# Polysketch attention and a gated FFN on one core: another way to load and spread S, and another order of the first loads

## The chip, the cores and the metric

The kernel runs on one core of a Trainium2 chip. The time is the device time in microseconds of one execution; a kernel's time is the median of several. Before the change it is 306.29 us (median of 4 runs, 305.91 to 307.54).

## What is computed

Two blocks follow each other. The first is attention with polynomial sketches, for 4 batches, 4 heads, 1088 tokens and a head dimension of 32; the second is a gated feed-forward block on the 4352 tokens with 128 features, with 1536 inner features.

```python
def phi(x):                                   # r = 8
    a = np.einsum('rd,bhsd->bhsr', S1, x)
    b = np.einsum('rd,bhsd->bhsr', S2, x)
    return np.einsum('bhsi,bhsj->bhsij', a, b).reshape(*x.shape[:-1], r * r)
q_p, k_p = (phi(q), phi(k))
kv = np.einsum('bhsf,bhsd->bhfd', k_p, v)
z = np.sum(k_p, axis=2)
num = np.einsum('bhsf,bhfd->bhsd', q_p, kv)
den = np.einsum('bhsf,bhf->bhs', q_p, z)[..., None] + 1e-06
x = (num / den), heads side by side            # (4352, 128)
gate = 1.0 / (1.0 + np.exp(-(x @ w_gate)))
out = gate * (x @ w_val) @ w_out
```

q, k and v come as float32. S1, S2 (8 x 32 each) and the three weights come as float64 (they were divided by a square root), so their bytes are twice those of float32 and the kernel turns them into float32 itself.

## The kernel before

The steady part is the feed-forward block. The 4352 tokens go through in nine chunks (eight of 512, one of 256). For each chunk and each of 12 blocks j of 128 inner features, TensorE makes the two products for gate and val (`w1`, L354, tile `wave`), ScalarE the sigmoid (L362), VectorE the product of both (L375, tile `g`), and TensorE adds the block's share of the output (`w2`, L311, tile `moeout`). The attention of batches 1 to 3 is laid in between these, a piece at a time (`slot`, L389 and following, and the loop at the end).

The attention of batch 0 has nothing to hide behind. It is written out by hand, and each engine runs its instructions in the order in which the code makes them (the schedule is manual). The first microseconds are therefore a chain:

- Loads. Queue of SyncE: `load_s` (L130), the second piece of k, the first of q, v in four transfers (`load_v`), then the weights of blocks 0 and 1 (`load_w(0)`: gate, val, out), the rest of q, and the weights of the other block pairs. Queue of ScalarE: the first piece of k alone. SyncE's queue waits, from the eighth transfer or so on, for the landing of the transfer eight before it.
- `warm` (L246): products of ones, made only to keep TensorE at work; three of 512 columns at the start (L256) and one of 256 later (L840). A float32 product runs as two passes.
- S. `load_s` reads each of S1 and S2 sixteen times, so that all 128 partitions hold a row (`sr_in`). `narrow` (L83) makes float32 of float64 in steps: on VectorE L97, L105 and L109, on ScalarE L101 and L117, on POOL L118, and on VectorE L121, which writes `sr`. Then VectorE transposes it in blocks of 32 (L784, `st`) and masks it by head into `sk` (L788). `sk` is the stationary side of `kps` (L442), the first real product; ScalarE spreads `st` into `s0` and `s1` (L804) for q.
- k and q. VectorE turns k (`turn_k`, L419, in two pieces) and q (`turn_q`, L430). `kps` makes k's sketches, VectorE turns them (`kab`, L452) and multiplies them out (`kp`, `outer`, L521). `ab` (L549, L568) does q's. `gram` (L465, L488) makes the sum z in another way, `dn` (L721, L740) the denominator and numerator, `kv0` (L629, tile `kvz`) k's features times v, `kvd` (L665) and `ndt` (L699, L712) bring that into the form for the numerator, and `divide` writes the first 512 tokens of `xT` (L767), with which the feed-forward block starts.
- Weights. `narrow_01` makes float32 of blocks 0 and 1: part 0 is gate and val of block 0, part 1 of block 1, part 2 the two of w_out. Its first steps stand on ScalarE and POOL (L101, L97) behind `gs` and `gh` of `gram`. `narrow_w` does the later blocks, a block per wave.

The order of `kv0`'s products before: the first 20 right behind `spread_z` (L821), ahead of `dps` (L721), and the last 16 in `rest` (L830), behind the second half of `outer`.

Of the kernel before, what the change touches and what calls it, by code (L numbers as in the profile page):

```python
# [8 lines left out]
F32 = mybir.dt.float32  # L9
I32 = mybir.dt.int32  # L10
U32 = mybir.dt.uint32
I64 = mybir.dt.int64
ALU = mybir.AluOpType
ACTF = mybir.ActivationFunctionType
MUL = ALU.mult

P = 128
# [3 lines left out]
def kernel(  # L21
# [12 lines left out]
    nc = tc.nc  # L34

    B, H, S, D = q.shape
    R = S1.shape[0]
# [6 lines left out]
    T = S // 32  # L44

    NJK = 9
    KBASE = [0, 9, 17, 25]
    assert T == 34
    TCH = 512
    tok_chk = [(o, min(TCH, NTOK - o)) for o in range(0, NTOK, TCH)]  # L50

    const = ctx.enter_context(tc.tile_pool(name="const", bufs=1))
# [3 lines left out]
    sbN = ctx.enter_context(tc.tile_pool(name="sbN", bufs=1))  # L56
# [5 lines left out]
    pso = ctx.enter_context(tc.tile_pool(name="pso", bufs=1, space=bass.MemoryType.PSUM))  # L62
# [17 lines left out]
    wide = S1.dtype == I64  # L80
    assert all((a.dtype == I64) == wide for a in (S2, moe_w_gate, moe_w_val, moe_w_out))

    def narrow(out, bits, eng, bank=None):  # L83

        n, m = out.shape[1:]
        lo, hi = bits[:, :, :, 0].bitcast(U32), bits[:, :, :, 1]

        def tmp(dt, tag, bufs):
            return sbN.tile([P, 3, P], dt, tag=tag, name=tag, bufs=bufs)[:, :n, :m]

        cap, tail = tmp(I32, "cap", 6), tmp(I32, "tail", 5)
        eng.tensor_scalar(  # L97
            out=cap.bitcast(F32), in0=hi.bitcast(F32), scalar1=122880.0, scalar2=-122880.0,
            op0=ALU.min, op1=ALU.max,
        )  # L100
        nc.scalar.activation(out=tail, in_=lo, func=ACTF.Copy, scale=2.0**-29)  # L101
        yield

        head = tmp(I32, "head", 3)
        nc.vector.tensor_scalar(  # L105
            out=head, in0=cap, scalar1=3, scalar2=0x3FFFFFF8,
            op0=ALU.logical_shift_left, op1=ALU.bitwise_and,
        )
        nc.vector.scalar_tensor_tensor(  # L109
            out=head, in0=cap, scalar=-0x40000000, in1=head, op0=ALU.bitwise_and, op1=ALU.bitwise_or  # L110
        )
        yield
        square = cap.bitcast(F32)
        if bank:
            square = pso.tile([P, 512], F32, tag=bank, name="square")[:, : n * m]
            square = square.rearrange("p (n m) -> p n m", n=n)
        nc.scalar.activation(out=square, in_=cap.bitcast(F32), func=ACTF.Square)  # L117
        nc.gpsimd.tensor_tensor(out=head, in0=head, in1=tail, op=ALU.add)  # L118
        yield

        nc.vector.scalar_tensor_tensor(  # L121
            out=out, in0=square, scalar=1.265625 * 2.0**-30, in1=head.bitcast(F32),
            op0=ALU.is_ge, op1=MUL,
        )
        yield

    sr = const.tile([P, 2, D], F32, tag="sr", name="sr")
    sr_in = const.tile([P, 2, D, 2], I32, tag="sr_in", name="sr_in") if wide else None

    def load_s():  # L130
        for n, s_ in enumerate((S1, S2)):
            rows = bass.AP(tensor=s_.tensor, offset=s_.offset, ap=[[0, P // R], [D, R], [1, D]])
            if wide:
                nc.sync.dma_start(
                    out=sr_in[:, n].rearrange("p d w -> p (d w)"), in_=rows.bitcast(I32)
                )
            else:
                nc.sync.dma_start(out=sr[:, n], in_=rows)


    w_sb = const.tile([P, 3, NJ, P], F32, tag="w_sb", name="w_sb")
    w_in = {}

    def load_w(n):
        j0, j1 = 2 * n, 2 * n + 2
        cs = slice(j0 * P, j1 * P)
        if wide:
            w_in[n] = raw.tile([P, 3, 2, P, 2], I32, tag="w_in", name="w_in")
        for i, src in enumerate((moe_w_gate, moe_w_val)):
            if wide:  # L150
                nc.sync.dma_start(
                    out=w_in[n][:, i].rearrange("p j m w -> p (j m w)"),
                    in_=src[:, cs].bitcast(I32),
                )
            else:
                nc.sync.dma_start(
                    out=w_sb[:, i, j0:j1].rearrange("p j m -> p (j m)"), in_=src[:, cs]
                )
        src = moe_w_out[cs, :].bitcast(I32) if wide else moe_w_out[cs, :]
        nc.sync.dma_start(  # L160
            out=w_in[n][:, 2].rearrange("p j m w -> p j (m w)") if wide else w_sb[:, 2, j0:j1],
            in_=src.rearrange("(j p) m -> p j m", p=P),
        )
# [28 lines left out]
    def load_rows(src, b, t, parts=((0, T, nc.sync),)):  # L192
        for t0, t1, eng in parts:
            eng.dma_start(
                out=t[:, t0:t1, :],
                in_=bass.AP(
                    tensor=src.tensor,
                    offset=src[b, 0].offset + t0 * D,
                    ap=[[T * D, P], [1, (t1 - t0) * D]],
                ),  # L200
            )

    def load_v(b):
        t = ld.tile([P, H, NJK, D], F32, tag="v", name="v")
        base = v[b, 0].offset
        for g in range(4):
            nc.sync.dma_start(
                out=t[32 * g : 32 * g + 32],
                in_=bass.AP(
                    tensor=v.tensor,  # L210
                    offset=base + KBASE[g] * D,
                    ap=[[T * D, 32], [S * D, H], [1, NJK * D]],
                ),
            )
        return t

    k_t, q_t, v_t = {}, {}, {}
# [11 lines left out]
            load_rows(q, b, q_t[b])  # L229

    new_kq(0)
    load_rows(k, 0, k_t[0], ((0, KBASE[2] + 1, nc.scalar),))
    load_s()
    load_rows(k, 0, k_t[0], ((KBASE[2] + 1, T, nc.sync),))
    load_rows(q, 0, q_t[0], ((0, T0, nc.sync),))
    v_t[0] = load_v(0)
    load_w(0)
    load_rows(q, 0, q_t[0], ((T0, T, nc.sync),))
    for n in range(1, NJ // 2):
        load_w(n)  # L240

    ones = const.tile([P, 32], F32, tag="ones")
    nc.vector.memset(ones, 1.0)
# [2 lines left out]
    def warm(*cols):  # L246
        t = psm.tile([P, 2, 512], F32, tag="wave", name="warm")
        one = [bass.AP(tensor=ones.tensor, offset=ones.offset, ap=[list(ones.ap[0]), [0, n]]) for n in cols]
        x = bass.AP(tensor=ones.tensor, offset=ones.offset, ap=[list(ones.ap[0]), [0, P]])
        for r in one:  # L250
            n = r.shape[-1]
            nc.tensor.matmul(out=t[:, 0, :n], lhsT=x, rhs=r, start=True, stop=True)  # L252

    sig0 = const.tile([P, 1], F32, tag="sig0")
    nc.scalar.activation(out=sig0, in_=ones[:, :1], func=ACTF.Sigmoid)
    warm(512, 512, 512)  # L256
    hm = const.tile([P, 2, R], F32, tag="hm")
    nc.vector.memset(hm, 0.0)  # L258
    for h in range(H):
# [1 line left out]
    ident = const.tile([P, P], F32, tag="ident")  # L261
# [9 lines left out]
    for c in range(2):  # L271
        rows = slice(64 * c, 64 * c + 64)
        nc.vector.tensor_reduce(
            out=m_col[rows, c],
            in_=ident[rows].rearrange("p (k j) -> p j k", j=R),
# [3 lines left out]
    for t, x in (  # L279
# [5 lines left out]
        out=e_sum,  # L285
        in_=bass.AP(
            tensor=e_row.tensor,
            offset=e_row.offset,
            ap=[list(e_row.ap[0]), [0, 2], [1, R], [0, R]],
        ),  # L290
# [332 lines left out]
    def kv0(j_list):  # L623
        if 0 not in KVZ:
            KVZ[0] = pso.tile([P, TCH], F32, tag="acc0", name="kvz")
        for j in j_list:
            kr = 64 if j == 0 else P
            for h in range(H):
                nc.tensor.matmul(  # L629
                    out=KVZ[0][32 * h : 32 * h + 32, :F],  # L630
                    lhsT=v_t[0][:kr, h, j, :],
                    rhs=KP[0][:kr, h // 2, j, h % 2, :],
                    start=(j == 1),
                    stop=(j == NJK - 1),
                    skip_group_check=True,
                )
# [78 lines left out]
    def dn(b, n, mid=None):  # L715
# [58 lines left out]

        return divide

    steps = narrow(sr, sr_in, nc.vector) if wide else iter(())
    turn_k(0, 0, KBASE[2] + 1)
    for _ in range(3):
        next(steps, None)  # L780
    turn_k(0, KBASE[2] + 1, T)
    next(steps, None)
    st_ = const.tile([P, 2, 4, R], F32, tag="st", name="st")
    nc.vector.transpose(  # L784
        out=st_.rearrange("p n u r -> p (n u r)"), in_=sr.rearrange("p n d -> p (n d)")
    )
    sk = const.tile([P, 2, 2, R], F32, tag="sk")
    nc.vector.tensor_tensor(  # L788
        out=sk,
        in0=st_[:, :, :2].rearrange("p n m r -> p m n r"),  # L790
        in1=bass.AP(
            tensor=hm.tensor, offset=hm.offset, ap=[list(hm.ap[0]), [R, 2], [0, 2], [1, R]]
        ),
# [24 lines left out]
    spread_z()  # L818
    for pi in range(2):
        outer(0, pi, 0, 5)  # L820
    kv0([1, 2, 3, 4, 0])  # L821
    mult00()
    mult10()
    mask_z()


    def rest(turn, rc, dT):
        for pi in range(2):
            outer(0, pi, 5, NJK)
        kv0(range(5, NJK))  # L830
        turn()
        nt = rc.shape[1] - 1
        nc.scalar.activation(out=rc[:, :nt], in_=dT[:, :nt, :2], func=ACTF.Identity, bias=eps)
        kvd(0)
        narrow_01(0, 1)
        narrow_01(0, 2)
        ndt(0)
# [100 lines left out]
```

## Time and profile before

| | us |
|---|---|
| median of 4 runs | 306.29 |
| the profiled execution | 307.54 |
| its span | 305.6 |
| TensorE busy | 297.5 (97%) |
| VectorE busy | 155.8 (51%) |
| ScalarE busy | 80.7 (26%) |
| POOL busy | 34.7 (11%) |
| `wave` products (L354) | 192.1 |
| `moeout` products (L311) | 105.5 |
| start of the first `kps` product | 7.11 |
| start of the first `wave` product | 16.97 |

Times of events are counted from the start of the span. The busy time of TensorE counts a pass until its modelled end; passes overlap, so the distance from the start of one pass to that of the next tells more than its length. A row of the clock tells which share of TensorE's full speed was granted; the stretch before the first record of a clock (here before 4.68 us) is shown as 1.00.

### The profile page before, as it was taken

Reading aid. Unit: us, or ns where it says so; the run is one execution under the profiler, and the core shown is the slowest. Engines: PE = TensorE matmul, PEld = TensorE weight load, DVE = VectorE, ACT = ScalarE, POOL = GpSimd, SP = SyncE. Lnnn points to the kernel's source line nnn. Section 1 sums busy time; section 2 is a strip of 40 time slices with the busy share of each in tenths; the row PEclk is TensorE's granted clock in tenths of the full one; section 3 lists DMA queues with packets and bytes.
Section 4 is the critical chain, followed back from the end, with each engine's and each line's share of the span. In section 5 each row is a group of like instructions: output and inputs, shape, how many; then the busy total and the mean of one; then the engine's idle time right before and its main releaser. Section 6 shows DMA issues by size and latency. Waiting matters only on the chain.

```text
span 305.6 us, 3603 instructions
## 1 busy us (share of the span) xinstructions
PE 297.5 (97%) x1361; PEld 137.2 (45%) x1361; DVE 155.8 (51%) x268; ACT 80.7 (26%) x150; POOL 34.7 (11%) x63
## 2 busy tenths in 40 slices
PE   6799999999999999999999999999999999999994
PEld 2454434444344444443444444434444444444683
DVE  6988888853846544563465542645232223222331
ACT  3455542221123222212222222221222222222220
POOL 2355550320000400000004100000000000000000
PEclk9989999999999999999999999999999999999999
DMA  6993531599502490341005950200011000100011
GB/s 194 349 344 72 133 118 42 115 170 171 156 0 34 108 222 20 69 150 42 0 5 130 169 81 2 35 0 2 0 17 17 0 0 8 28 0 0 7 28 17
DMA packets 29841, 23.35 MB, mean 76 GB/s; under 512 B 21184, under 2 KB 24768, under 8 KB 29824
## 3 DMA queue, kind: packets, MB, share of 16 engines
q1 hardware_dynamic: 25600, 15.54, 19.0%
q0 software_dynamic: 3456, 7.09, 12.8%
q10 hardware_dynamic: 768, 0.51, 0.7%
q8 instruction: 10, 0.16, 0.2%
q14 instruction: 7, 0.06, 0.1%
HBM read 19.86 MB, written 3.26 MB: 76 GB/s over the span
## 4 chain that ended last, share of the span: by engine, by line
PE 87%; DMA 6%; DVE 2%; POOL 1%; SPq 1%; issue 1%; ACT 0%; DVEq 0%; ACTq 0%
PE wave L354 53%; PE moeout L311 28%; DMA bq<-dq 4%; PE nps L740 2%; PE dps L721 1%; DMA kq<-in_k_dram 1%; PE kps L442 1%; PE kvz L643 1%; DMA out_dram<-o_sb 1%; PE cqps L588 1%; POOL qp L612 1%; POOL bq L612 0%; DVE qp L621 0%; SPq L332 0%; DVE kp L521 0%
## 5 line engine op out<-in xcount | busy, mean ns | idle before, releaser
L354 PE MATMUL wave<-xT,w_sb 128*128 128x512 f32 (+1 forms) x436 | 192.1, 567 | 0.0
L375 DVE TENSOR_TENSOR g<-wave,sg 128x512 f32<-128x512 f32 x102 | 70.4, 690 | 130.4 <-ACT sg L362 130.1
L354 PEld LDWEIGHTS wave<-xT,w_sb 128*128 128x128 f32 x436 | 83.4, 191 | 93.1 <-issue 88.7
L362 ACT ACTIVATE sg<-wave 128x512 f32<-128x512 f32 x102 | 60.9, 597 | 202.7 <-PE wave L354 202.7
L311 PE MATMUL moeout<-g,w_sb 128*128 128x512 f32 (+1 forms) x216 | 105.5, 576 | 0.1
L311 PEld LDWEIGHTS moeout<-g,w_sb 128*128 128x128 f32 x216 | 39.5, 190 | 44.1 <-issue 38.4
L612 POOL DMA_DIRECT2D qp<-dq x12 | 7.0, 587 | 109.5 <-DMA dq<-cq 109.5
L118 POOL TENSOR_TENSOR head<-head,tail 128x384 int32<-128x384 int32 (+2 forms) x14 | 13.4, 960 | 19.5 <-DVE head L109 14.7
L621 DVE TENSOR_TENSOR qp<-qp,bq 128x1152 f32<-128x1152 f32 (+1 forms) x7 | 9.1, 1295 | 4.2 <-DMA bq<-dq 4.2
L521 DVE TENSOR_TENSOR kp<-kab 128x1152 f32<-128x1152 f32 (+2 forms) x10 | 10.9, 1110 | 0.0
L109 DVE SCALAR_TENSOR_TENSOR head<-cap,head 128x384 int32<-128x384 int32 (+2 forms) x14 | 7.5, 538 | 0.5
L321 DVE STREAM_TRANSPOSE o_sb<-moeout 128x512 f32<-128x512 f32 (+1 forms) x9 | 6.1, 680 | 2.6 <-PE moeout L311 2.5
L612 POOL DMA_DIRECT2D bq<-dq x12 | 6.9, 577 | 0.5 <-DMA out_dram<-o_sb 0.2
L252 PE MATMUL warm<-ones 128*128 128x512 f32 (+1 forms) x8 | 5.9, 887 | 1.0 <-DVE hm L258 1.0
L101 ACT ACTIVATE tail<-w_in 128x384 int32<-128x384 uint32 (+1 forms) x13 | 6.5, 521 | 1.0 <-DMA w_in<-in_moe_w_val_dram 1.0
L97 POOL TENSOR_SCALAR cap<-w_in 128x384 f32<-128x384 f32 (+1 forms) x13 | 6.5, 506 | 0.5 <-DMA w_in<-in_moe_w_val_dram 0.5
L121 DVE SCALAR_TENSOR_TENSOR w_sb<-square,head 128x384 f32<-128x384 f32 (+1 forms) x11 | 5.6, 518 | 1.7 <-POOL head L118 1.6
L767 DVE TENSOR_TENSOR xT<-nps,rb 128x576 f32<-128x576 f32 (+2 forms) x9 | 5.9, 661 | 0.8
L740 PE MATMUL nps<-qp,nd 64*32 64x256 f32 (+1 forms) x128 | 6.0, 432 | 0.4 <-ACT nd L712 0.4
L756 DVE STREAM_TRANSPOSE rb<-rc 128x576 f32<-128x576 f32 (+2 forms) x9 | 6.1, 681 | 0.3
L419 DVE STREAM_TRANSPOSE kT<-kq 128x1088 f32<-128x1088 f32 (+2 forms) x5 | 5.4, 1072 | 1.2 <-DMA kq<-in_k_dram 1.2
L430 DVE STREAM_TRANSPOSE qT<-kq 128x512 f32<-128x512 f32 (+1 forms) x8 | 5.8, 720 | 0.0
(72 smaller groups left out, 83.3 us busy)
## 6 DMA issues: line engine op xcount, KB each, us to landing
qp<-dq POOLq DMA_DIRECT2D x12, 288.0 KB, 8.2
bq<-dq POOLq DMA_DIRECT2D x12, 288.0 KB, 8.4
v<-in_v_dram SPq DMA_DIRECT2D x16, 144.0 KB, 5.0
kq<-in_k_dram SPq DMA_DIRECT2D x3, 544.0 KB, 3.9
kq<-in_q_dram SPq DMA_DIRECT2D x3, 544.0 KB, 5.4
w_in<-in_moe_w_gate_dram SPq DMA_DIRECT2D x6, 256.0 KB, 5.8
w_in<-in_moe_w_val_dram SPq DMA_DIRECT2D x6, 256.0 KB, 6.1
w_in<-in_moe_w_out_dram SPq DMA_DIRECT2D x6, 256.0 KB, 6.6
```

Of the source, the lines that this page charges most:

```text
L97: eng.tensor_scalar(out=cap.bitcast(F32), in0=hi.bitcast(F32), scalar1=122880.0, scalar2=-122880.0, op0=ALU.min, op1=ALU.max,)
L101: nc.scalar.activation(out=tail, in_=lo, func=ACTF.Copy, scale=2.0**-29)
L109: nc.vector.scalar_tensor_tensor(out=head, in0=cap, scalar=-0x40000000, in1=head, op0=ALU.bitwise_and, op1=ALU.bitwise_or)
L118: nc.gpsimd.tensor_tensor(out=head, in0=head, in1=tail, op=ALU.add)
L311: nc.tensor.matmul(out=moe["acc"][:, :tw], lhsT=w_sb[:, 2, j, :], rhs=g[:, jj, :tw], start=(j == 0), stop=(j == NJ - 1),)
L354: nc.tensor.matmul(out=wv[:, which, jj * tw + o : jj * tw + o + tp], lhsT=w_sb[:, which, j0 + jj, :], rhs=xT[:, t0 + o : t0 + o + tp], sta ...
L362: nc.scalar.activation(out=sg, in_=wv[:, 0], func=ACTF.Sigmoid)
L375: nc.vector.tensor_tensor(out=g, in0=wv[:, 1], in1=sg, op=MUL)
L521: nc.vector.tensor_tensor(out=KP[b][:, pi, j0:j1].rearrange("p j m (i l) -> p (j m) i l", i=R), in0=bass.AP(tensor=a0.tensor, offset=a0.of ...
L612: get.dma_start(out=t[64 * c : 64 * c + 64, n * H * W1 : (n + 1) * H * W1], in_=bass.AP(tensor=d0.tensor, offset=d0.offset, ap=rows + [[1, ...
L621: nc.vector.tensor_tensor(out=q0, in0=q0, in1=half(BQ[b], n), op=MUL)
L740: nc.tensor.matmul(out=t[32 * h : 32 * h + 32, c, :w], lhsT=ND[b][rows, 32 * h : 32 * h + 32], rhs=half(QP[b], n)[rows, 2 * (h % 2) + h // ...
```

## The change

S is read once: S1 onto partitions 0 to 7 and S2 onto 8 to 15 (`s_in`). `narrow` works on these 16 partitions, and its last step writes four copies side by side (`s4`, 16 x 4 x 32). One TensorE product with the identity turns and spreads them in one go into PSUM (128 x 16, in bank `acc0`), where `sk` and the two copies of ScalarE read it. The block transposition on VectorE is gone. The first three steps of `narrow` stand ahead of the first turn of k on VectorE instead of behind it, and the step that writes `s4` stands ahead of the second turn.

The second piece of k goes onto ScalarE's queue, behind the first. `load_w` is split: gate and val of blocks 0 and 1 stand ahead of v on SyncE's queue, and w_out behind v as before. The first 20 products of `kv0` move behind `dps`. The first `warm` has two products instead of three.

```diff
-    def narrow(out, bits, eng, bank=None):
+    def narrow(out, bits, eng, bank=None, copies=None):
-        n, m = out.shape[1:]
+        p, n, m = bits.shape[:3]
...
+        head = head.bitcast(F32)
+        if copies:
+            square, head = (
+                bass.AP(tensor=x.tensor, offset=x.offset, ap=[list(x.ap[0]), [0, copies], [1, m]])
+                for x in (square, head)
+            )
         nc.vector.scalar_tensor_tensor(
-            out=out, in0=square, scalar=1.265625 * 2.0**-30, in1=head.bitcast(F32),
-            op0=ALU.is_ge, op1=MUL,
+            out=out, in0=square, scalar=1.265625 * 2.0**-30, in1=head, op0=ALU.is_ge, op1=MUL
         )
...
-    sr = const.tile([P, 2, D], F32, tag="sr", name="sr")
-    sr_in = const.tile([P, 2, D, 2], I32, tag="sr_in", name="sr_in") if wide else None
+    s4 = const.tile([2 * R, 4, D], F32, tag="s4", name="s4")
+    s_in = const.tile([2 * R, 1, D, 2], I32, tag="s_in", name="s_in") if wide else s4[:, :1]
     def load_s():
         for n, s_ in enumerate((S1, S2)):
-            rows = bass.AP(tensor=s_.tensor, offset=s_.offset, ap=[[0, P // R], [D, R], [1, D]])
+            rows = s_in[R * n : R * n + R, 0]
             if wide:
-                nc.sync.dma_start(
-                    out=sr_in[:, n].rearrange("p d w -> p (d w)"), in_=rows.bitcast(I32)
-                )
+                nc.sync.dma_start(out=rows.rearrange("p d w -> p (d w)"), in_=s_.bitcast(I32))
...
     new_kq(0)
-    load_rows(k, 0, k_t[0], ((0, KBASE[2] + 1, nc.scalar),))
     load_s()
-    load_rows(k, 0, k_t[0], ((KBASE[2] + 1, T, nc.sync),))
+    load_rows(k, 0, k_t[0], ((0, KBASE[2] + 1, nc.scalar), (KBASE[2] + 1, T, nc.scalar)))
     load_rows(q, 0, q_t[0], ((0, T0, nc.sync),))
+    load_w_in(0)
     v_t[0] = load_v(0)
-    load_w(0)
+    load_w_out(0)
     load_rows(q, 0, q_t[0], ((T0, T, nc.sync),))
     for n in range(1, NJ // 2):
-        load_w(n)
+        load_w_in(n)
+        load_w_out(n)
...
-    warm(512, 512, 512)
+    warm(512, 512)
...
-    steps = narrow(sr, sr_in, nc.vector) if wide else iter(())
+    if wide:
+        steps = narrow(s4, s_in, nc.vector, copies=4)
+        for _ in range(3):
+            next(steps)
     turn_k(0, 0, KBASE[2] + 1)
-    for _ in range(3):
-        next(steps, None)
+    if wide:
+        next(steps)
...
     turn_k(0, KBASE[2] + 1, T)
-    next(steps, None)
-    st_ = const.tile([P, 2, 4, R], F32, tag="st", name="st")
-    nc.vector.transpose(
-        out=st_.rearrange("p n u r -> p (n u r)"), in_=sr.rearrange("p n d -> p (n d)")
-    )
+    st_ = pso.tile([P, TCH], F32, tag="acc0", name="st")
+    nc.tensor.matmul(
+        out=st_[:, : 2 * R],
+        lhsT=s4.rearrange("p g d -> p (g d)"),
+        rhs=ident[: 2 * R, : 2 * R],
+        is_transpose=True,
+        start=True,
+        stop=True,
+    )
+    st_ = st_[:, : 2 * R].rearrange("p (n r) -> p n r", n=2)
...
     for pi in range(2):
         outer(0, pi, 0, 5)
-    kv0([1, 2, 3, 4, 0])
     mult00()
...
     def rest(turn, rc, dT):
+        kv0([1, 2, 3, 4, 0])
         for pi in range(2):
             outer(0, pi, 5, NJK)
```

## The prediction

> **What bounds the kernel now.** I read the page first, then the chain of waits of the first 30 us, then the same stretch engine by engine in order of time, then windows with the granted clock.
>
> ```profile
> span 305.6 us, 3603 instructions
> PE   6799999999999999999999999999999999999994
> PE 87%; DMA 6%; DVE 2%; POOL 1%; SPq 1%; issue 1%; ACT 0%; DVEq 0%; ACTq 0%
> ```
>
> From the third slice on (15 us) TensorE is never idle, and its work there is not touched by the diff. So the change is worth what it moves in the first 17 us, before the first `wave` matmul (16.97 us), and no more. The chain of waits there:
>
> ```profile
> 1.49 0.58 SPq L134
> 2.07 0.05 issue
> 2.12 3.59 DMA kq<-in_k_dram
> 5.71 0.02 issue
> 5.73 0.08 DVE kT L419
> 5.81 0.56 issue
> 6.37 0.19 DVE sr L121
> 6.58 0.26 DVE st L784
> 6.86 0.20 DVE sk L788
> 7.11 0.72 PE kps L442 x16
> ```
>
> Columns are start, length, what. The second piece of k is issued at 2.12, behind the two S transfers on SyncE's queue, and lands at 5.71. Then VectorE does four things one after another (turn of k, `sr`, `st`, `sk`) and `kps` starts at 7.11.
>
> ```profile
> 1.16 1.28 ACT L255 ACT_TABLE_LOAD   x1 [1.16 <-PEq L922]
> 3.58 0.78 DVE L419 STREAM_TRANSPOSE kT<-kq 128x576 f32<-128x576 f32 x1 [0.89 <-DMA kq<-in_k_dram]
> 3.68 0.34 PEld L252 LDWEIGHTS warm<-ones 128*128 128x128 f32 x1 [0.52 <-issue]
> 4.53 0.26 PEld L252 LDWEIGHTS warm<-ones 128*128 128x128 f32 x1 [0.52 <-issue]
> 4.78 0.20 DVE L97 TENSOR_SCALAR cap<-sr_in 128x64 f32<-128x64 f32 x1 [0.42 <-DMA sr_in<-in_S_dram]
> 10.72 1.11 ACT L101 ACTIVATE tail<-w_in 128x256 int32<-128x256 uint32 x3 [0.99 <-DMA w_in<-in_moe_w_val_dram]
> ```
>
> S lands at about 4.7, a microsecond after the first k. And ScalarE's first weight step at 10.72 waits 0.99 for val: a front end that comes earlier by more than that would run into the weights.
>
> ```profile
> 8.50:10.20 1.70, 1.53 (x55) 0.91 (x52) 1.70 (x4) 1.19 (x3) 0.39 (x1) 1.00 1.01 319
> 12.00:14.00 2.00, 1.55 (x40) 0.74 (x40) 1.97 (x5) 0.37 (x2) 0.02 (x1) 1.00 1.06 383
> 16.00:17.20 1.20, 1.20 (x7) 0.97 (x4) 1.04 (x3) 0.27 (x1) 1.20 (x3) 0.50 1.07 376
> 17.20:19.00 1.80, 1.80 (x7) 1.45 (x7) 1.73 (x6) 0.39 (x1) 0.77 (x2) 0.69 1.06 376
> ```
>
> Columns: stretch and length, then busy time of PE, weight loads, DVE, ACT, POOL, then clock, DMA share, GB/s. From 8 to 16 VectorE is full (1.70 of 1.70, 1.97 of 2.00), so its chain moves as a block with `sk`. And the clock: its records change at 4.68, 14.92 and 18.33, so half speed is granted from 14.92 for 3.41 us; the full stretch before it is three times 3.41.
>
> **The change part by part.**
>
> *Second k piece to ScalarE's queue, S small.* On SyncE one issue of 0.59 goes, and the two S transfers shrink from 128 rows of 256 B each to 8. On ScalarE one issue of about 0.39 (the row of the first k piece) is added at 1.13, so the table load and the sigmoid that follow it end at 3.05 instead of 2.65; ScalarE's next work is `tail` on S, not before 3.1, which hides it. If S came at 2.7 it would cost 0.35 there. k2 is issued 1.0 earlier. Landing, best case: it keeps its 3.59 and lands at 4.7; worst: 5.71 as now, because q's first piece (issued at 2.75 now, about 1.7 then, its two S and k issues ahead being shorter or gone) takes its half of the DMA engines. By bytes, k and q together are 800 KB against 864 KB with S, all landed at 6.6 now, so 6.1 for the later of the two. I take 5.0 for k2, 6.1 for q.
>
> *S itself.* The second S lands at 4.67 now, with k's first piece ahead of it. A load of 2 KB has no row here; the shortest way from issue to landing among the small transfers of the trace is 1.5 us and their median 2.0 (the stores of `o_sb`). Issued at about 1.2 it lands between 2.7 and 4.67 (no gain from size). I take 3.4, nearer to the short rows since its bytes are 1/128 of k's, but behind k1, which keeps the engines until 3.56.
>
> *VectorE in the new order.* Three S steps (now 4.78, 5.01, 5.24, ending 5.46: 0.68 in all) stand ahead of the turn of k. From 3.4: end 4.1. Turn of the first k piece (0.78): 4.1 to 4.9. POOL's `head` (now 0.47 from the third step to its end) is ready at 4.6, hidden under that turn. The step that writes the four copies (16x128, costed at 0.18 by the `sr` row): 4.85 to 5.05. Turn of k2 (0.71): 5.05 to 5.75. The transposition on VectorE (0.24) goes; in its place one TensorE product of 16 columns, bounded below by nothing and above by `ndps` (128 columns, 0.33) plus a weight load (0.34): 5.05 to 5.4, or 5.75 at the worst, both under the turn of k2. TensorE must be free at 5.05: two warm matmuls, four passes 0.85 apart from 0.96, end by 4.4 to 4.7; a third would have held it until 5.63. `sk` at 5.75 plus 0.20, `kps` at 6.0 against 7.11: **1.1 earlier**. With k2 at 5.71: sk at 6.45, gain 0.4. With S at 4.67 the turn of k1, now queued behind the three steps, waits until 5.46; copies by 6.4, k2's turn until 7.1, kps at 7.35: a loss of 0.25. With S at 2.7 and k2 at 4.7 the turn of k1 starts at 3.58, the copies are written by 4.55 and k2's turn ends at 5.4: gain 1.45. Reading `st` from PSUM: `zm`, which reads PSUM, takes 0.21 against sk's 0.19; nothing. The turn of q stands behind `sk` on VectorE: q at 6.1 lets it run 6.15 to 6.85, and `kab`, behind it, needs kps until 6.7. So kab starts at 6.85 against 7.93: still 1.1.
>
> *Gate and val ahead of v.* In the profile w_val is the transfer with 1952 KB up to its end and lands at 10.64; v ends there after 1440 KB at 9.09. In the new order val ends after 1312 KB, so about 8.3; ScalarE wants it at 9.6 (10.72 less 1.1): the 0.99 wait goes, which alone would have eaten most of the gain. v now ends after 1888 KB: about 10.4.
>
> *The first 20 `kvz` products behind `dps`.* They now fill TensorE from 10.71 to 11.6 while it waits for `zb`. Moved, `dps` stands at 10.85 to 11.45, then all 36 products follow: 0.68 for the first 20 and 0.6 for the rest, with a tail of 0.2, so 12.95 against 12.75 (13.87 less 1.1) if nothing were moved. v at 10.4 is covered by dps by 1.0; if v came at 12, everything behind, `kvd` first, would be late by 0.6. `kvd` waits on ScalarE behind `rc`, which ends 12.83, so the move costs **0.1 to 0.2** at `nps`. VectorE reaches its `xT` step at 14.9, nps ends at 14.75 to 15.1: first half of xT at 15.0 to 15.2, against 16.13. Gain there: 0.95.
>
> *Into the waves.* The 256-column warm matmul and the first 8 passes follow. If the half clock lies where it lies in this execution (14.92 to 18.33), an earlier start means more passes at 0.43 instead of 0.22: start 15.7, sixth pass at 17.8, eighth ended at 18.75, against 19.37: 0.62 gained. If the half-clock stretch moves along with the work, 0.95 stays. I take **0.8**. Behind that TensorE is bound until the end, and nothing gives it back: the weights of later blocks arrive at 370 GB/s, 768 KB each 2.1 us, against 5.2 us in which TensorE uses them.
>
> Sum: 1.1 - 0.15 - 0.15 = 0.8. The profiled execution took 307.54 (span 305.6 and 1.9 around it), so 306.7 for it; it is the longest of the four runs shown, and their median is 306.29, so 305.5.
>
> **A rule against the change.** The rows: passes 0.85 apart from 0.96 to 4.53, then full speed from 4.68; later `wave` passes lie 0.43 apart. So the clock opened 3.7 us after the first warm pass, with 5.1 us of warm passes issued; the change leaves 3.4. In TensorE: Matmul & The Clock Gate, the Part 1 section and the table under Why this matters for your kernels, the Trainium skill says that the gate opens after a free-running window of about 3.4 us has been busy, and advises at least 4 us of warm-up. By that rule the shortened warm-up may miss the window, depending on its phase, and the sum would be that of the second rival below. By the rows, the 3.41 us before 4.68 were busy throughout; with passes that end at 4.4 they would be busy for 3.1. Also, DMA: Bandwidth & Descriptors, section Issuing engines are not separate DMA queues, says that transfers issued from two engines interleave on the same 16 DMA engines and only issue time is saved; by that k2 would land nearer 5.7, and the sum would be that of the third rival.
>
> **The rivals.**
>
> 1. *Waves at full clock.* The half-clock stretch of 14.92 to 18.33 is put down by what TensorE did before it; the products are moved and shifted, so it may fall elsewhere. Without it j=0's eight passes take 1.72 from 15.4 and VectorE's steps bind: its `g` at 20.20 has 0.54 of idle time before it and could start at 18.6, a gain of 1.6. For: only one such stretch in the profile. Against: the move of kvz leaves a new hole on TensorE ahead of dps. Time 304.7 and down to 304.2.
>
> 2. *Half clock in the front (the slow side).* The warm-up of four passes doesn't open the clock, and kps, aps, gram, bps, dps, kvz run at half: a group of eight passes took 0.43 at half clock (`nps`) against 0.24 to 0.27 at full (`aps`, `kps`). Six such groups up to bps, two of dps, gram's and kvz's small passes at twice their spacing: 6 x 0.2 + 0.35 + 0.3 + 0.6 = about 2.4, of which VectorE's full stretch hides little. With the half clock kept into the waves as now, the time is 305.5 + 2.4 = 307.9. It decides from the point where the clock is at half when kps starts. For: four passes of 0.85 last no longer than the one half-clock stretch that the profile shows (3.41). Against: 3.1 of the 3.41 us before 4.68 stay busy.
>
> 3. *The change doesn't do what it says: k2 lands no earlier*, sharing with q. Gain 0.4 at kps less 0.15: 306.0.
>
> **How the numbers follow.** The forecast (305.5, own range 304.9 to 306.1) has 0.40, rival 1 has 0.20, rival 2 has 0.22, rival 3 has 0.18. A measurement of this kernel can tell about 0.5% from no change, 1.5 us: 304.76 to 307.82. Forecast and rival 3 lie inside; of rival 1 about 0.16 lies below, and 0.04 of the forecast with an early S and k2; of rival 2 about 0.13 lies above. So faster 0.20, same 0.67, slower 0.13. The range of 304.3 to 307.7 takes in the bounds of k2 and S (a gain of 1.45 and a loss of 0.25 at kps) and about half of rival 2.
>
> **What would show it.** Right: kps at 5.8 to 6.2 just behind sk; the turn of k2 right behind the copies step; kvz without a wait for v; no wait of ScalarE for val; the first wave pass near 15.7. Wrong: `kT` waiting for k beyond 5.1 (rival 3); kps passes in groups of 0.43 and no clock record before 6 us (rival 2); no half clock between 15 and 19 (rival 1). The whole is wrong if the stretch behind 22 us differs in length, since I give it no part.

## The result, and the profile after

| | before | after |
|---|---|---|
| median, us | 306.51 (305.75 to 308.86, 79 runs) | 308.37 (304.91 to 311.85, 53 runs) |
| ratio, 95% interval | | 1.0044 [1.0032, 1.0056] |
| profiled execution / its span | 307.54 / 305.6 | 308.13 / 305.2 |
| first `kps` / first `dps` product | 7.11 / 11.96 | 5.93 / 10.79 |
| first `wave` / first `moeout` product | 16.97 / 21.28 | 17.12 / 21.16 |

The changed kernel is slower: the medians lie 1.86 us (0.6%) apart, and 308.37 is above the range of the forecast (up to 307.7) and above the 307.82 that I had set as the upper bound to no change. The ratio, here and in all that follows, leaves out executions more than 1.5% above the fastest of their kernel (9 of the changed kernel's), so it is smaller than that of the medians. The changed kernel's first product comes 1.18 us earlier and its first wave no earlier at all. The page of the changed kernel (the span, the clock in 40 slices, the chain that ended last):

```profile
span 305.2 us, 3600 instructions
PEclk9789999999999999999999999999999999999999
PE 96%; DVE 1%; DMA 1%; issue 0%; ACT 0%; SPq 0%; DVEq 0%
```

The chain now runs through TensorE almost alone, while DMA had 6% before. The half clock lies in the second and third slices (7.6 to 22.9 us), where before it lay behind 14.92. The chain of waits of the changed kernel (start, length, what):

```profile
1.20 2.42 DMA s_in<-in_S_dram
...
4.32 0.32 DVE kT L428
4.64 0.30 issue
4.95 0.24 DVE s L127
5.18 0.62 DVE kT L428
5.81 0.09 DVE sk L813
5.89 0.04 issue
5.93 0.72 PE kps L451 x16
...
10.79 0.84 PE dps L730 x8
11.62 2.28 PE kvz L638 x72
...
15.07 1.11 PE nps L749 x16
16.18 1.15 PE warm L261 x2
17.33 3.80 PE wave L363 x12
```

S lands at 3.62. The second turn of k follows the copies step at once: k is not waited for. Up to `dps` all stands where it was forecast. Then 72 passes of `kvz` take 2.28. The windows of the changed kernel show why (stretch and length, busy time of PE, weight loads, VectorE, ScalarE, POOL, then the granted clock, DMA share, GB/s):

```profile
8.00:11.00 3.00, 1.48 (x38) 0.84 (x42) 2.97 (x7) 1.21 (x4) 1.28 (x3) 1.00 1.08 289
11.00:14.00 3.00, 2.86 (x80) 1.99 (x72) 2.90 (x9) 0.83 (x3) 1.22 (x2) 0.52 1.06 377
14.00:18.00 4.00, 3.40 (x22) 1.91 (x23) 2.44 (x7) 2.16 (x7) 1.72 (x3) 0.51 1.06 372
```

The clock fell at 11.10 and came back at 17.93, 6.83 us later: just the stretch from `kvz` to the first waves. Ahead of it TensorE had been busy for 1.48 of 3.00.

**Three kinds of execution.** I say that the clock *opens* when the granted clock goes from half to full, and *falls* when it goes back. Every execution lists its span and its mean granted clock. A half clock of 6.83 us takes 3.41 of 305 off the mean, so it reads 0.989; one of 3.41 us reads 0.994. A mean of 0.997 or more has two meanings, since the time before the first clock record counts as 1.00: the clock opened in the warm-up and *held*, or it *opened late*. The span tells them apart (I put the border at 306.2; the profiles of either kind lie at 303.8 to 304.2 and at 306.6 to 307.5). Below 0.997 the clock opened early and *fell* again. Executions with a span between 304.2 and 306.6 lie between the profiles and are placed by the border alone (one of e3 lies on it and is counted as late). The runs of all kernels by this reading (for before, the 100 that ran beside the experiments; for after, all 54 executions listed, one more than the median takes in):

| kernel | warm products | first `kvz` products | gate/val | held | fell | late | ratio |
|---|---|---|---|---|---|---|---|
| before | 3 | ahead of `dps` | behind v | 72 | 26 | 2 | 1 |
| after | 2 | behind | ahead | 5 | 24 | 25 | 1.0044 [1.0032, 1.0056] |
| e12_warm1 | 1 | behind | ahead | 0 | 0 | 6 | 1.0128 [1.0097, 1.016] |
| e1_warm3 | 3 | behind | ahead | 5 | 6 | 1 | 1.0005 [0.9982, 1.0028] |
| e2_before_warm2 (before) | 2 | ahead | behind | 0 | 5 | 4 | 1.0096 [1.0064, 1.0128] |
| e3_products_back | 2 | ahead | behind | 3 | 5 | 4 | 1.0022 [0.9994, 1.0049] |
| e5_warm3_products_back | 3 | ahead | behind | 12 | 0 | 0 | 0.9974 [0.9959, 0.999] |
| e7_warm3_v_first | 3 | behind | behind | 5 | 7 | 0 | 1.0005 [0.9974, 1.0036] |
| e8_loads_changed | 3 | ahead | ahead | 3 | 9 | 0 | 1.0021 [0.9995, 1.0046] |
| e9_filled | 3, holes filled | behind | ahead | 12 | 0 | 0 | 0.998 [0.9957, 1.0003] |
| e10_back_filled | 3, two holes filled | ahead | behind | 10 | 2 | 0 | 0.9985 [0.9969, 1.0] |
| e11_short_fill | 2.5, one filler | ahead | behind | 8 | 2 | 2 | 0.9984 [0.9949, 1.0019] |
| e16_before_moved (before) | 3 | behind | behind | 6 | 6 | 0 | 1.0 [0.9977, 1.0022] |

The kernel before fell in 7 of 32, 8 of 28, 5 of 17 and 6 of 23 executions beside the four groups of experiments, so the groups can be compared.

In the changed kernel the medians of the three kinds are 306.02, 307.65 and 309.25 us; in the kernel before 306.48, 307.15 and 308.73. The 306.02 rests on five executions, 304.91 to 307.85. With the changed kernel's medians and the shares of before the mean would be 0.72 x 306.02 + 0.26 x 307.65 + 0.02 x 309.25 = 306.51, against 306.70 for before worked out likewise; with its own shares it is 308.24. So by this estimate the loss is one of shares: 1.7 us by kinds of execution, less 0.2 for what the change does within a kind.

### The profile page after: what moved, and what is told of

Read it like the earlier page. It is cut to its first block, busy times and chain, and to the rows that moved or that the text cites. A ratio compares the mean times of both kernels' runs of the same rounds, so it can differ in the third digit from the quotient of the medians.

```text
span 305.2 us, 3600 instructions
## 1 busy us (share of the span) xinstructions
PE 296.9 (97%) x1360; PEld 137.3 (45%) x1360; DVE 155.2 (51%) x267; ACT 80.7 (26%) x150; POOL 34.7 (11%) x63
## 4 chain that ended last, share of the span: by engine, by line
PE 96%; DVE 1%; DMA 1%; issue 0%; ACT 0%; SPq 0%; DVEq 0%
PE wave L363 58%; PE moeout L320 30%; PE nps L749 2%; PE dps L730 2%; PE kvz L652 1%; PE kps L451 1%; DMA s_in<-in_S_dram 1%; PE kvz L638 1%; PE cqps L597 1%; PE warm L261 0%; PE ndps L708 0%; DVE kT L428 0%; PE gram L474 0%; PE kvz L661 0%; DVE qp L577 0%
## 5 line engine op out<-in xcount | busy, mean ns | idle before, releaser
L730 PE MATMUL dps<-qp,zb 128*32 128x256 f32 (+1 forms) x64 | 5.5, 415 | 1.2 <-DVE zb L520 1.2
L261 PE MATMUL warm<-ones 128*128 128x512 f32 (+1 forms) x6 | 4.8, 944 | 1.0 <-DVE hm L267 1.0
```

The lines of the kernel that those rows point to most:

```text
L730: nc.tensor.matmul(out=dps[32 * h : 32 * h + 32, :w], lhsT=zb[b % 2][:, h, :], rhs=half(QP[b], n)[:, 2 * (h % 2) + h // 2, :], start=True, ...
```

## The experiments

**How many warm products?** The change made three products of 512 columns into two. e1 puts the third back, e12 takes one more away, e2 does to the kernel before what the change did; e4, e13 and e14 are the changed kernel again, for its profile alone.

```diff
-    warm(512, 512)              # after
+    warm(512, 512, 512)         # e1
+    warm(512)                   # e12
-    warm(512, 512, 512)         # before
+    warm(512, 512)              # e2
```

> The changed kernel with the third warm product given back. Theory A (the shorter warm-up opens TensorE's clock late in many executions, and that is the whole loss): median 305.5 to 306.1, ratio to the kernel before 0.997 to 0.999, and the spread of the runs as narrow as before's (some 3 us instead of 7). Theory B (the moved products leave TensorE idle ahead of dps, and the clock is lost there): no help, median about 308, ratio 1.003 to 1.006. Theory C (the earlier front end is paid back in the loads): also about 308.

> The kernel before with two warm products instead of three, nothing else. Theory A: slower by 1 to 3 us in the median (307.5 to 309.5) with a wide spread (up to 310 or more). Theories B and C: no change within 0.3 us, ratio 0.999 to 1.001, since the third product is on no path (TensorE is idle from 5.63 to 7.11).

> The changed kernel once more, for a second profiled execution. Theory A: the clock's first record lies later than the 4.28 of the first profile in about half of the executions; where it does, kps, aps and bps show groups of eight passes at 0.43 instead of 0.24 to 0.27, and the span is 306 to 308. If it opens at about 4.3 to 5.5 again, a half-clock stretch should begin at the end of a 3.41 us step between 8 and 12.

> The changed kernel with one warm product only. Theory A: the clock can't open before the real products come, so nearly all runs fall into the upper group of the changed kernel's times (308.8 to 309.8), with kps, aps, bps, dps, kvz, nps at half and the clock's first record at 13 us or later; median 308.8 to 310, narrower than the changed kernel's 7 us. Rival (that upper group comes from the transfers of batch 1's q, some 60 to 79 us into the span, and not from the clock): no shift, median 308.0 to 308.5 with the changed kernel's spread.

> The changed kernel once more, for a profile of the upper group of its times (309 and more). Theory A: an execution of 309 has the clock's first record behind 8 us and the first wave product at 18 us or later, and nothing lost behind it. Rival: the first wave product at 17 as in the two profiles so far, and TensorE idle for 2 us or more near 78 us, waiting for the last gather of batch 1.

> As the run before it: one more execution of the changed kernel, to be placed by where its clock opens.

Measured: 310.45 with one product (309.22 to 312.79), 308.37 with two, 307.06 with three (305.49 to 308.81); in the kernel before, 309.77 with two against 306.52 with three. e4 took 306.80 (span 305.0; opened at 4.57, half from 7.98 to 14.80), e14 308.41 (first clock record at 15.93), e13 309.51 (at 20.56). Three of the expectations were missed: e1 lies between what its theories gave, e2 and e12 lie above their ranges. Of e2's profiled execution (311.36) some 3 us are lost far behind the front (last section), so its time is not the clock's alone. The third profile of the changed kernel, e13, by the timeline of TensorE (start, length, what; idle time ahead and its releaser in brackets):

```profile
5.97 1.22 PE L451 MATMUL kps<-kT,sk 64*32 64x288 f32 x16 [0.41 <-DVE sk L813]
7.11 1.16 PE L558 MATMUL aps<-qT,s 32*64 32x256 f32 x16
...
12.51 1.08 PE L730 MATMUL dps<-qp,zb 128*32 128x256 f32 x8 [1.36 <-DVE zb L520]
13.34 2.49 PE L638 MATMUL kvz<-kp,v 128*32 128x64 f32 x72
...
19.09 4.33 PE L363 MATMUL wave<-xT,w_sb 128*128 128x256 f32 x12
23.45 1.12 PE L320 MATMUL moeout<-g,w_sb 128*128 128x512 f32 x2
```

The same view of e12, with one warm product:

```profile
5.96 1.22 PE L451 MATMUL kps<-kT,sk 64*32 64x288 f32 x16 [0.41 <-DVE sk L813]
...
19.08 4.33 PE L363 MATMUL wave<-xT,w_sb 128*128 128x256 f32 x12
23.44 1.12 PE L320 MATMUL moeout<-g,w_sb 128*128 128x512 f32 x2
```

They agree to 0.01 us. So this execution of the changed kernel is one in which the warm-up did nothing: 16 passes of `kps` take 1.22 instead of 0.72, `aps` 1.16 instead of 0.69, and the first `moeout` stands at 23.45. With one warm product all 6 executions are of this kind, with two 25 of 54, with three 1 of 12 (and none of 36 in e5, e7 and e8 below). By the ratios (1.0044 [1.0032, 1.0056] against e1's 1.0005 [0.9982, 1.0028]) the third product takes back the larger part of the loss. But e1 only comes back to the time of before: with the clock opened, 6 of its 12 fall again.

Between two of its changes in the front the clock stays for 3.41, 6.83, 10.24 or, in e10, 13.65 us in all profiles: whole multiples of 3.41. So I count in steps of 3.41. The early openings lie at 3.91 to 7.10, each with a step of 3.41 us ahead of it in which TensorE was busy; the emptiest is e2's, 2.83 of 3.41. Two windows of e2 (columns as above), up to its opening and behind it:

```profile
1.91:5.32 3.41, 2.83 (x4) 0.67 (x2) 2.06 (x8) 1.00 (x3) 0.00 (x0) 1.00 0.74 238
5.32:8.74 3.42, 0.78 (x24) 0.28 (x26) 2.28 (x7) 0.65 (x3) 0.53 (x2) 1.00 1.04 241
```

Two products keep TensorE busy from 0.96 to 4.74. A step that holds 2.83 of this must end between 3.79 and 5.32: a band of 1.53 in 3.41. My estimate from these rows is therefore that 45% of executions open early, if steps begin at any point alike; 29 of 54 (54%) did. The other profiles with two products agree: after, e4 and e3 opened inside this band (4.28, 4.57, 5.10), while in e13 and e14 the steps, counted back from the late opening, end outside of it (3.49 and 5.69). e2's second row is a step of 0.78, at whose end the clock fell.

The Trainium skill, TensorE: Matmul & The Clock Gate, Part 1: The HAM clock gate, says that the window is free-running, so that the point of opening varies from run to run. These runs agree that it varies, but the page gives the variation as 0.5 us; here the early openings spread over 3.91 to 7.10, and a missed one came only at 15.93 and 20.56 in the profiles.

**Which order makes it fall?** e3 undoes the order of products and loads and leaves two warm products; e5 does so with three, so that only the S and k parts of the change are left. e7 keeps the products' move alone, e8 the order of loads alone, each with three. e16 is the kernel before with the products moved.

```diff
     # e3, e5, e7: v ahead of gate and val again
-    load_w_in(0)
     v_t[0] = load_v(0)
+    load_w_in(0)
     # e3, e5, e8: products ahead of dps again
+    kv0([1, 2, 3, 4, 0])
     mult00()
...
     def rest(turn, rc, dT):
-        kv0([1, 2, 3, 4, 0])
     # e5, e7, e8
-    warm(512, 512)
+    warm(512, 512, 512)
     # e16, in the kernel before: the two kv0 lines the other way round
```

> The changed kernel with the first 20 kvz products back ahead of dps and v back ahead of gate and val; two warm products as changed. Theory A: still slow with a wide spread, 307.5 to 309. Theory B: the loss is gone, 305.5 to 306. Theory C: 305.5 to 306 too.

> Only the S and k parts of the change: third warm product, kvz order and load order as before. Theory A: like the run with the third warm product alone, 305.3 to 306.2. Theory B: 305.3 to 306, and clearly better than the run with the third warm product alone. In both, kps at about 6.0 and ScalarE's first weight step waiting for val until about 10.6.

> The changed kernel with the third warm product and with v back ahead of gate and val, but the 20 kvz products still behind dps. Theory B (on top of A: moving the products leaves TensorE so idle ahead of dps that the clock falls): as the run with the third warm product alone, 306.7 to 307.4. Rival: it is the load order, with v behind gate and val, that cost the difference; then 305.7 to 306.2 as in the run with both undone.

> The changed kernel with three warm products and the products back ahead of dps, but gate and val still ahead of v. If the load order is free: as the run with both undone, 305.7 to 306.2. If v's later landing (about 10.4) is waited for by kvz, TensorE stands until then and dps, zb's follower, comes 0.5 to 0.8 late: 306.3 to 306.8.

> The kernel before with its first 20 kvz products moved behind dps, nothing else. Theory B: TensorE idles ahead of dps, the clock falls earlier or for longer in part of the executions; median 306.9 to 307.8, spread up to 309, two groups. Rival (the products' place costs only its 0.1 to 0.2 us on the path): 306.5 to 306.8, spread as before's.

Measured: e3 308.01, e5 305.95 (305.3 to 306.64), e7 306.88, e8 307.66, e16 307.07 (before 306.88 in that comparison). e5 beats both kernels and is the version to keep. Its timeline of TensorE:

```profile
6.00 0.23 PE L803 MATMUL st<-ident,s 16*128 16x16 f32 x1
6.51 0.72 PE L451 MATMUL kps<-kT,sk 64*32 64x288 f32 x16 [0.28 <-DVE sk L813]
...
16.02 3.71 PE L363 MATMUL wave<-xT,w_sb 128*128 128x256 f32 x12 [0.15 <-DVE xT L776]
20.08 1.12 PE L320 MATMUL moeout<-g,w_sb 128*128 128x512 f32 x2 [0.35 <-DVE w_sb L127]
```

The third warm product holds TensorE until 6.00, so `st` and with it `kps` are 0.58 later than in the changed kernel (6.51 against 5.93); in exchange the clock is open and stays so in 12 of 12. Beside it, e7 falls in 7 of 12 and e8 in 9 of 12. So either order, alone, is enough to lose the clock in part of the executions. Where it holds, the orders cost little: the medians of the held executions are 305.95 (e5), 305.77 (e1), 305.99 (e7) and 306.32 (e8), so the place of the products is not what costs the 1 to 2 us. In time only e8 is told apart from e5 (1.0021 [0.9995, 1.0046] against 0.9974 [0.9959, 0.999]); e7's interval overlaps with e5's. In e16, with the front of before, the move shows no effect on the time, and its 6 falls of 12 are not told apart from 6 of 23 of before beside it. e8 lies above the 306.3 to 306.8 expected for a wait for v. The products do wait for v, which the loads put later, as its timeline shows:

```profile
10.44 0.90 PE L638 MATMUL kvz<-kp,v 128*32 128x64 f32 x40 [0.48 <-DMA v<-in_v_dram]
```

**Can the holes be filled?** e9 keeps the whole change and adds, beside the third warm product, products of ones, whose results nothing reads: 256 columns ahead of `spread_z`, twice 256 behind it, 128 behind `kvz` and 128 behind `ndps`. e10 adds the last two to e5. e11 is e5 with a third warm product of half the size and 128 columns behind `st`.

```diff
+    fill(st_bank, 256)
     spread_z()
+    fill(st_bank, 256, 256)
...
         kv0(range(5, NJK))
+        fill(KVZ[0], 128)          # e9, e10; a like one behind ndps
-    warm(512, 512, 512)            # e11, against e5
+    warm(512, 512, 256)
+    fill(st_, 128)
```

> The changed kernel, its product and load order kept, with the third warm product and idle products of ones laid into the holes of TensorE (256 columns ahead of spread_z, 512 behind it, 128 behind kvz, 128 behind ndps). They do no useful work. Theory A and B together: the clock never falls, 305.0 to 306.0 with a spread under 2 us. Rival (the moved products cost by their place on the path, not by the clock): no better than 306.7, or worse by the time of the fillers.

> The S and k parts alone with three warm products, and idle products of 128 columns behind kvz and behind ndps. Theory A and B: the clock stays open more surely than in the run without them, so 305.5 to 306.0 and a spread under 1.5 us. If they only stand in the way: 0.2 to 0.4 above 305.95.

> The S and k parts alone (products and load order as before), with warm products of 512, 512 and 256 columns, and one of 128 columns right behind the st product. Theory A: TensorE is as busy up to kps as with three full ones, but st comes 0.5 earlier (5.3 to 5.6 instead of 6.0), so 305.2 to 305.9, a little below the 305.95 of the run with three. If the gate needs the full third product, 306.5 to 308 with a wide spread.

Measured: e9 306.17 (305.72 to 307.15), e11 306.0 (305.41 to 309.21, two of its 12 opened late and two fell), e10 306.42 (306.06 to 311.65); all three a little above what was expected. Where the clock holds already, fillers bring nothing: e10 is 0.47 behind e5, though the intervals overlap. Nor do fillers behind `kvz` and `ndps` make it safe: two of e10's 12 executions fell, at 311.08 and 311.65. The second is the profiled one. There k's second piece landed only at 7.64 (6.48 after its issue), TensorE stood idle for 1.85 ahead of `kps` at 8.51, and the clock fell at 10.51. Why k came late, no run shows. In e9 the fillers do what they are for. A window of e9:

```profile
8.00:12.00 4.00, 3.79 (x88) 2.44 (x87) 3.97 (x9) 1.65 (x5) 1.91 (x4) 1.00 1.07 307
```

The timeline of TensorE in e9:

```profile
10.78 0.64 PE L740 MATMUL dps<-qp,zb 128*32 128x256 f32 x8 [0.21 <-DVE zb L528]
11.21 1.55 PE L646 MATMUL kvz<-kp,v 128*32 128x64 f32 x72
...
15.69 3.71 PE L371 MATMUL wave<-xT,w_sb 128*128 128x256 f32 x12
19.74 1.13 PE L328 MATMUL moeout<-g,w_sb 128*128 128x512 f32 x2 [0.34 <-DVE w_sb L127]
```

TensorE is busy for 3.79 of the 4 us in which the changed kernel lost its clock; `dps` stands where it stood there (10.78), `kvz` takes 1.55 where it took 2.49 in e13 at half clock, and the first wave starts at 15.69, at the 15.7 of the forecast. None of its 12 executions fell, where e1, the same without the fillers, fell in 6 of 12 and opened late in one. In time alone the two are not told apart (0.998 [0.9957, 1.0003] against 1.0005 [0.9982, 1.0028]).

**When does it fall?** The step of the changed kernel at whose end its clock fell:

```profile
7.69:11.10 3.41, 1.89 (x59) 1.07 (x44) 3.38 (x7) 1.52 (x5) 1.28 (x3) 1.00 1.08 287
```

The step of e9 with the same work and the fillers:

```profile
7.32:10.73 3.41, 3.25 (x61) 2.12 (x60) 3.38 (x8) 1.84 (x5) 1.29 (x3) 1.00 1.08 275
```

Counted so from the opening, the falls came behind steps with 1.89 (after), 1.89 (e1), 2.17 (e3), 2.02 (before), 2.35 (e16), 2.00 (e10), 2.50 (e4) and 0.78 (e2) of TensorE busy; in the profiles that held the emptiest step had 2.14 (e7), 2.39 (e8), 2.40 (e5), 2.42 (e11) and 2.94 (e9). The two sets overlap, and first steps of 1.93 (before), 2.02 (e16) and 2.27 (after) led to no fall. So a sparse step is what goes with a fall, and filling the sparse steps ended the falls in e9; a threshold is not shown.

## Why the prediction was wrong

The forecast was 305.5 with a range up to 307.7; measured were 308.37. The step that failed is the one that took the granted clock as given: two warm products were to open it as three had, and the hole that the moved products and loads leave on TensorE was priced only with 0.1 to 0.2 us at `nps`, and with nothing for the clock. What the runs showed in its place: 25 of 54 executions opened late (median 309.25) and 24 fell (307.65); only five held (306.02). With three products 1 of 12 opened late, and with the holes filled as in e9 none fell.

- **S, k and VectorE's order: right.** S landed at 3.62 (forecast 3.4), the copies step ran 4.95 to 5.18 (4.85 to 5.05), the turn of k2 from 5.11 without a wait (5.05), `st` lay under it with 0.23 (0.35), `sk` stood at 5.74 (5.75) and `kps` at 5.93 (6.0). The gain there was 1.18 against 1.1, and rival 3 (k2 no earlier) didn't happen.
- **Gate and val ahead of v: half right.** ScalarE's first weight step no longer waits for val, and `kvz` doesn't wait for v behind `dps`. ScalarE's third step now waits 2.38 us for w_out, which the split put behind v; it starts at 11.59. What was not weighed is that the order of loads and the order of products make TensorE's work sparser, and what that costs: by e7 and e8, the clock.
- **The products behind `dps`, "0.1 to 0.2 at `nps`": wrong where the clock falls.** `dps` came at 10.79 (10.85), but the products ended at 13.90 instead of 12.95 and `nps` started at 15.07, where it should have ended. With the clock held (e9) the working holds: first wave 15.69 against 15.7. That it fits so closely is in part luck: e9 has a third warm product and fillers, and opened at 3.91, the earliest of all; the held profiles lie at 15.58 to 16.06.
- **"Into the waves", 0.8: the term that failed in the profiled execution.** I let the half clock of 14.92 to 18.33 stay or move along, and took 0.62 or 0.95 as the gain. It became twice as long and began at 11.10, ahead of `kvz`; the first wave went from 16.97 to 17.12, the first `moeout` gained 0.12. The hole ahead of `dps` that I named against rival 1 lies in the step ahead of the fall.
- **The likeliest case took four warm passes as enough.** Rival 2 (half clock in the front) had 0.22. It came in 25 of 54 executions, and I had read the one phase of one profile as the kernel's: 3.1 busy of 3.41 holds for steps that end at 4.68, and by the estimate above (45%) a missed opening was about as likely as an early one. The rule of the skill that I had cited against the change was right as a warning, but its 4 us are no safe figure here: e11's warm-up lasts 4.63 us in its profile, and two of its 12 executions opened late.
- **Rival 2's price was too small.** I gave it 2.4 and 307.9; its executions have a median of 309.25 and a span of 307.4, against 304.2 for the changed kernel's held ones: 3.2. Between e9 and e13, `dps` is 1.73 later (my terms up to there: 1.5), `nps` 2.60 (my terms from `dps` to there: 0.95, measured 0.87), the first wave 3.40. Missing was mainly the last 0.80, `nps` and the 256-column warm product at half clock, which I had taken to be at half already in the base.
- **The base.** The median of four runs (306.29) was 0.22 below that of 79 (306.51). The profiled execution of before (clock 0.993, 307.54) was itself one that fell, as 26 of 100 do; of its 1.25 above the median 0.67 is what lies between the medians of the two kinds (307.15 and 306.48). Its half clock at 14.92 wasn't part of the kernel's usual course, and the gain that I reckoned around it could be none in the 72 that held.
- **The stretch behind 22 us, to which I gave no part: right.** From the first `moeout` to the end it lasts 284.0 to 284.2 in 13 of the 16 profiles, with the clock held, fallen or opened late alike; 284.3 in the kernel before, 284.7 in e1, 287.0 in e2 (below).

What stays open: why within the held kind the changed kernel gains only 0.46 (306.02 against 306.48) of the 1.18 at `kps`. No profile shows the kernel before with its clock held, so the wave's start there isn't known. Among the held profiles an earlier `kps` brings little for the wave: e9 and e7 start `kps` at 5.92 and 6.95, 1.03 apart, and the first wave at 15.69 and 16.06, 0.37 apart (the two kernels differ in their loads and fillers too).

## What to carry to other kernels

A warm-up is part of the critical path's price, not slack: before it is cut, count how much of one clock step its busy time still fills for every phase, and put the uncertain share into the chances. Work that looks idle-filling on TensorE (the first 20 products ahead of `dps`) may be part of what keeps the clock; a move of it is costed with the busy share of the 3.4 us that it leaves. And where a median moves by some tenths of a per cent, sort the single executions by mean clock and span before reading any one profile: the kernel may be a mixture, and its profile one draw from it.

## What the runs showed of the hardware

A step with TensorE busy throughout did not always open the gate. In e13 the step from 6.90 to 10.31 (steps counted back from the opening at 20.55) holds `kps`, `aps`, `gram` and `bps`, whose weights take 32 or 64 rows; the one ahead of the opening holds `nps`, warm passes and waves:

```profile
6.90:10.31 3.41, 3.41 (x76) 1.63 (x68) 2.29 (x4) 1.82 (x5) 0.46 (x2) 1.00 1.09 218
...
17.14:20.55 3.41, 3.41 (x22) 2.10 (x23) 2.22 (x7) 1.62 (x4) 0.95 (x2) 1.00 1.05 371
```

Both are busy for 3.41 of 3.41, at half clock by their passes (the 1.00 stands for "no record yet"). The same goes for the step from 8.74 in e2, that from 8.51 in e3 and that from 10.51 in e10: full, at half clock, with products of that kind, and no opening at the end. Yet steps that hold `dps` and `kvz` instead opened with 2.94 (e16) and 3.03 (e14), and one of e10 with 3.06 did not. So the busy time that the profile counts does not decide alone. That small products count for less is one reading; no run tests it.

A late gather can cost a second time. In e2 the gathers for batch 1 are issued some 2 us later, and the last of them lands at 79.3 (before: 75.34). The chain of waits of the kernel before:

```profile
62.20 13.14 DMA bq<-dq
75.47 1.36 DVE qp L621
```

The same chain in e2:

```profile
64.12 15.18 DMA bq<-dq
...
79.42 1.36 DVE qp L621
```

A window of e2:

```profile
74.00:82.00 8.00, 5.33 (x34) 1.72 (x33) 2.51 (x5) 1.19 (x2) 0.00 (x0) 1.00 0.90 141
```

TensorE is idle for 2.67 of the 8 us there in e2 (0.10 in the kernel before): the rest of its loss, 287.0 behind the first `moeout` instead of 284. The last gather took 15.18 instead of 13.14, so half of its delay of 4 us is the late issue and half a longer way. The late issue alone does not do it: e12 issues its last gather later still, at 64.83, none of its gathers takes over 12.2, and TensorE is busy for all of the same 8 us. What made the way longer in e2 no run here shows.
